# Attention heads scored singly in 32x32 tiles, the last tokens of four heads packed into one tile, values spread through DRAM, softmax sums by half, no instruction padding

## The chip, the cores and the metric

The kernel runs on one core of one Trainium2 chip. The metric is the device time of one execution in microseconds (us). A core has a matrix engine (TensorE, PE in the profile, with its weight loads as PEld), a vector engine (DVE), an activation engine (ACT), GpSimd (POOL), and a queue-only engine (SyncE, SP) that issues most DMAs here. Each engine runs its own instructions in order and waits for the others on semaphores. Matmuls write to PSUM, the accumulation memory, and the other engines read it there; a bank in this text is a stretch of 512 float32 columns, the last dimension of the code's PSUM tiles. Everything else lies in SBUF, 128 partitions wide.

## The reference

Four blocks, each added to its own input: attention A, gMLP B, A, B, all on 2048 tokens of 512 features in bfloat16.

```python
def _A_ref(x, mem0, Wq, Wk, Wv, Wo, seg_len):       # H, Dh = 32, 128;  M, seg = 8, 32
    mask = (idx[:, None] < M) | (idx[:, None] >= idx[None, :])
    mem = mem0
    for s in range(n_seg):                           # 64 segments
        h = jnp.concatenate([mem, x[:, s * seg_len:(s + 1) * seg_len, :]], axis=1)   # 40 rows
        q, k, v = (jnp.einsum('btd,dhe->bhte', h, W) for W in (Wq, Wk, Wv))
        scores = jnp.einsum('bhqe,bhke->bhqk', q, k) * Dh ** (-0.5)
        p = _softmax(jnp.where(mask[None, None], scores, -1000000000.0), axis=-1)
        o = jnp.einsum('bhqk,bhke->bhqe', p, v)
        o = jnp.einsum('bhte,hed->btd', o, Wo)
        mem = o[:, :M, :]                            # the memory of the next segment
        outs.append(o[:, M:, :])
x = x + _A_ref(_layernorm(x), A_mem0, A_Wq, A_Wk, A_Wv, A_Wo, A_seg_len)
x = x + _B_ref(_layernorm(x), B_w_in, B_w_sp, B_b_sp, B_w_out)
x = x + _A_ref(...)
x = x + _B_ref(...)
```

The eight memory rows of a segment's output are the first eight rows of the next segment's input, so the 64 segments of an A block run strictly one after the other. That is 128 segments in all. `_B_ref` (a gelu, a layernorm, a 2048x2048 product over tokens and an output product) is not touched by the change.

## The kernel before

**A segment.** `a_block` runs `segment(s, ...)` 64 times. A segment has 40 rows: 8 of memory, 24 first tokens and 8 last tokens. Only 32 of them pass through the segment's own projections: the memory and the first 24 tokens, transposed in `hA`. The last 8 tokens do not depend on the memory as inputs, so their queries, keys and values are computed ahead for the four segments of a 128-token block at once, 32 rows at a time in `hB`. These are `QTB`, `KTB` and `VB` ("old" or "front" in the profile's names, after the buffers that hold them).

The 32 heads are handled as two halves, r=0 and r=1, of 16 heads. In this order on PE:

- q0 and k0 (`qk`, L690, PSUM tile `psm`): 16 pairs of weight load and matmul each, in tiles of 128x32. ACT casts the result to rows (L867), DVE transposes the rows to `QQ` and `KA` (L871).
- q1 and k1 (`qk_halves`, L880, `psm2`) in two halves of 256 columns each, every half in a PSUM tile of its own; casts L883, transposes L886.
- v0 (`v_mm`, `psV`), cast to `VA` by DVE (L960).
- scores (`scores`, L904), one PSUM tile `psS` for each r. Two heads share a 64-column tile, so each matmul also computes the products of one head's keys with the other's queries, which the mask removes. Per r there are 8 matmuls with `KA` (80 columns) and 8 with `KTB` (32 columns); the 32 rows of `KTB` are the last tokens of all four segments of the block, of which the mask keeps the right ones.
- `exps` (ACT, L911, 448 columns for each r) and `close` (DVE, L914), which multiplies by the 0/1 mask `maskN`.
- v1, cast to `VA` by ACT (L971), and fill units (below).
- The softmax sums: matmuls of `E` with ones. `psM` (L976) has those of the memory rows, `psD` (L985) those of the tokens. Between them stands PV for r=0 (`pv`, L930) into its tile `psO`; PV for r=1 follows in another `psO`.
- Division as Exp(-Ln(sum)) on ACT: `Rm` from psM (L989, L990), `Rt` from psD (Ln L995, 1024 columns; Exp L1003, 512 for each r).
- DVE scales the memory rows of psO by `Rm` into `uT` (L997); the output pass `wo_pass` (L747, 32 heads x 4 tiles = 128 pairs) multiplies `uT` by Wo into `pw`.
- `tok_out` (L944) and `last_out` (L948) scale the token rows by `Rt`. They go to the next segment's `uT` and to a buffer of last tokens, so a segment's tokens pass Wo with the next segment's memory rows.
- `build_hA`: DVE puts the memory rows of `pw` into the next input (copy_predicated, L820) and transposes it to `hA` (L821), which releases the next q0. `store_o` copies `pw` out (L826) and stores it (L827).

**Fill units.** Work that does not depend on the memory stands in the gaps of a segment: `b_units` (the last tokens' projections for the next block) and `y_part` (the last tokens' output product). `fill()` issues the next unit. There are two calls after v1, one before the output pass and one after it.

**Padding.** A page of PE instructions is taken as 256 (`PE_PAGE`). `fills_of` and `pads_of` split matmuls of the projections into two halves of the columns until each segment has 3 x 256 PE instructions, a weight load and a matmul counting as one each.

**Order.** PE, DVE and ACT run in the order in which the code issues the work (`manual_schedule` with `ORDERED`). PSUM tiles come from tagged pools with one buffer each: `accA`, `accB`, `att`, and `attO[0]`, `attO[1]`; a new tile of a tag waits until the one before it has been read.

**SP.** The layernorm rows of a later block go to DRAM and back in other shapes (`rows.apply`: L202 `xn_d`, L205 `preB` x4, L212 `pre` x4), `ln_x` is loaded (L192), `o_sb` is stored (L827), and finished rows are added to x: `y_load` (L220, L222), `y_add` on DVE, `y_norm` with its store (L237).

Of the kernel before, what the change touches and what calls it, by code (L numbers as in the profile page):

```python
# [14 lines left out]
P = 128  # L15
DM = 512
KT = 4
# [11 lines left out]
PE_PAGE = 256  # L29
SEGMENT_PE = 600  # L30
FILL_AHEAD = ((0, 0, 0, 106), (0, 0, 0, 50))
OLD_SIZES = (H * P, 8 * DH, H * 32, H * 32)
ORDERED = {mybir.EngineType.PE, mybir.EngineType.DVE, mybir.EngineType.Activation}

# [21 lines left out]
def _consts(ctx, tc, c, b_sp):  # L56
# [13 lines left out]
    maskf = tmp.tile([P, 4, 112], F32, name="maskf")  # L70
    nc.gpsimd.memset(maskf[:], 0.0)
    for g in range(2):
        for sl in range(2):
            q = 32 * (2 * g + sl)
            nc.gpsimd.memset(maskf[q:q + 32, :, 40 * sl:40 * sl + 40], 1.0)
            nc.gpsimd.memset(maskf[q:q + 32, :, 80 + 16 * sl:96 + 16 * sl], 1.0)

            blk = maskf[q:q + 32, :, 40 * sl + 8:40 * sl + 32]
            nc.gpsimd.affine_select(out=blk, in_=blk, compare_op=ALU.is_ge, fill=0.0, base=8,
                                    pattern=[[0, 4], [1, 24]], channel_multiplier=-1)  # L80

            for lo, step in ((8, 1), (0, 0)):
                blk = maskf[q:q + 32, :, 80 + 16 * sl + lo:88 + 16 * sl + lo]
                nc.gpsimd.affine_select(out=blk, in_=blk, compare_op=ALU.is_ge, fill=0.0, base=0,
                                        pattern=[[-8, 4], [0, 8]], channel_multiplier=1)
                nc.gpsimd.affine_select(out=blk, in_=blk, compare_op=ALU.is_ge, fill=0.0, base=0 if step else 7,
                                        pattern=[[8, 4], [step, 8]], channel_multiplier=-1)
    maskN = cp.tile([P, 4, 112], BF16, name="maskN")
# [5 lines left out]
    for g in range(2):  # L94
        nc.vector.memset(onesG[64 * g:64 * g + 64, g, :], 1.0)
# [378 lines left out]
def kernel(  # L474
# [32 lines left out]
    rows = _Rows(nc, rp, xd, xn_d, xb_d, o_d, x_in)  # L507
    with tc.manual_schedule(engines=ORDERED):
# [89 lines left out]
class _Ahead:  # L598
# [12 lines left out]
    def chunks(self, two):  # L611
# [3 lines left out]
        VB = VB.rearrange("p (r n) -> p r n", r=2)  # L615
        for pair in ((0, 2), (1, 3), (4, 5)):
# [7 lines left out]
            for k, j in enumerate(pair):  # L624
                if j >= 4:
                    nc.scalar.copy(VB[:, j - 4, :], ps[:, k, :])
                    continue
                r = self.rows.pool.tile([P, DM], BF16, name="ln_xn", bufs=2)
                nc.scalar.copy(r[:], ps[:, k, :])
                nc.vector.transpose(out=(QTB, KTB)[k][:, 512 * (j % 2):512 * (j % 2) + 512], in_=r[:])  # L630
# [3 lines left out]
def a_block(tc, c, rows, front, MV_in, RS_in, MV_out, RS_out, ahead, wo, S, first):  # L634
# [6 lines left out]
    with ExitStack() as ctx:  # L641
# [4 lines left out]
        for i in range(2):  # L646
            at, v = 0, list(front.old()) if i == 0 else []
            for n in OLD_SIZES if i == 1 else ():
                v.append(old.tile([P, n], BF16, name=f"old{at}")[:])
                at += n  # L650
            oBr[i] = v[0].rearrange("p (h t) -> p h t", h=H)
            VBr[i] = v[1].rearrange("p (r i e) -> p r i e", r=2, i=4)
# [12 lines left out]
        attO = [_Tagged(ps_pool, f"attO{r}", 1) for r in range(2)]  # L665
# [10 lines left out]
        def mm_chunk(ps, lhs, rhs, kts=range(KT), halved=0):  # L676

            for kt in kts:
                for cg in range(4):
                    k, r = 4 * kt + cg, rhs(kt, cg)  # L680
                    n = halved * (k + 1) // 16 - halved * k // 16
                    o = ps[32 * cg:32 * cg + 32, :]
                    if n and len(r.shape) == 4:
                        parts = [(o.rearrange("p (a b) -> p a b", a=2)[:, a].rearrange("p (i c) -> p i c", i=2), r[:, 2 * a:2 * a + 2]) for a in range(2)]
                    elif n:
                        parts = [(o[:, 256 * a:256 * a + 256], r[:, 256 * a:256 * a + 256]) for a in range(2)]
                    else:
                        parts = [(o, r)]
                    for a, (o, r) in enumerate(parts):
                        nc.tensor.matmul(o, lhsT=lhs(kt, cg), rhs=r, start=(kt == 0 and a == 0), stop=(kt == KT - 1 or halved > 0),  # L690
                                         tile_position=(0, 32 * cg), skip_group_check=halved > 0)
# [4 lines left out]
        QQr = [pers.tile([P, 2, 16, 40], BF16, name=f"QQ{i}") for i in range(NKQ)]  # L696
        uT = [pers.tile([P, H, 32], BF16, name=f"uT{i}") for i in range(2)]
# [5 lines left out]
        def ln_turn(tb):  # L703
            blk_state[tb] = dict(hB=ahead.turn(tb), KTB=KTBr[tb % 2], QTB=QTBr[tb % 2], VB=VBr[tb % 2])


# [8 lines left out]
        def b_units(tb, early=False):  # L715
            bs = blk_state[tb]

            for k, j in enumerate((0, 2, 1, 3, 4, 5)):
# [10 lines left out]
                def out(k=k, j=j, ps=ps):  # L729
                    if j >= 4:  # L730
                        nc.scalar.copy(bs["VB"][:, j - 4].rearrange("p i e -> p (i e)"), ps)
                        return
# [10 lines left out]
        def wo_pass(po, lhs, heads=range(H)):  # L743
            for h in heads:
                n = h // 8 * 8 + 2 * (h % 4) + h // 4 % 2
                for cg in range(4):
                    nc.tensor.matmul(po[32 * cg:32 * cg + 32, 0:128], lhsT=lhs[:, n, :], rhs=wo_rhs(h, cg),  # L747
                                     start=(h == 0), stop=(h == H - 1), tile_position=(0, 32 * cg))
# [6 lines left out]
        def wo_last(parts, pwB):  # L755

            for k, units in enumerate(parts):
                for t, (src, h) in enumerate(units):
                    n = h // 8 * 8 + 2 * (h % 4) + h // 4 % 2
                    nc.tensor.matmul(pwB[32 * t:32 * t + 32, :], lhsT=src[:, n, :], rhs=wo.head(h).rearrange("p (kt g el) -> p g kt el", kt=4, g=4),  # L760
# [49 lines left out]
        def prep_segment(s):  # L810
# [4 lines left out]
            seg_state[s] = dict(QQ=QQ, KTB=bs["KTB"], VB=bs["VB"])  # L815
# [13 lines left out]
        def fills_of(s):  # L829

            if s < 0:
                return FILL_AHEAD[not first]
            if s % 4 == 0:
                return (8, 8, 16, 32) if s // 4 > 3 else (0, 0, 0, 0)
            return (8, 8, 16, 32)

        def pads_of(s):

            n = (3 * PE_PAGE - SEGMENT_PE - fills_of(s - 1)[3] - sum(fills_of(s)[:3]) + 1) // 2
            pads = dict(q0=0, k0=0, q1=16, k1=16, v0=0, v1=0)  # L840
            n -= 32
            for chunk, most in (("k0", 8), ("v0", 8), ("v1", 8), ("v0", 16), ("k0", 16), ("v1", 16), ("q0", 16)):
                k = min(n, most - pads[chunk])
                pads[chunk] += k
                n -= k
            assert n == 0
            return pads

        def segment(s, fill, spare1, spare2, tail):
            tb, j4 = s // 4, s % 4  # L850
            pads = pads_of(s)
            st = seg_state.pop(s)
            QQ, KTB, VB = st["QQ"], st["KTB"], st["VB"]
# [7 lines left out]
            E = segp.tile([P, 2, 4, 112], BF16, name="E")  # L861

            def qk(j):
                ps = (accB if j < 2 else accA).tile([P, 512], F32, name="psm")
                mm_chunk(ps, lambda kt, cg: hA_cur[:, kt, :], lambda kt, cg: qk_rhs(w, j, kt, cg), halved=pads[("q0", "q1", "k0", "k1")[j]])
# [303 lines left out]
```

## Time and profile before

| | |
|---|---|
| median of 3 runs (lowest, highest) | 1766.57 us (1764.97, 1771.19) |
| span of the profiled execution | 1737.3 us |
| PE busy | 1682.0 us, 97% |
| PEld busy | 1271.2 us, 73% |
| DVE busy | 1167.4 us, 67% |
| ACT busy | 1111.3 us, 64% |
| POOL busy | 121.4 us, 7% |
| DMA queue q1: packets, MB, share of 16 engines | 182728, 90.38, 21.2% |

The span is the time from the first to the last instruction of one profiled execution; the medians are of whole executions and include what lies around it. Busy time is the time in which an engine has at least one instruction under way. Matmuls are pipelined, so rows of the timeline overlap, and the start of a row says more than its length. In a row of a timeline stand: start in us, length in us, engine, line, operation, output<-input by the program's names, shapes, and how many instructions are grouped (x); in brackets the idle time before and what released the engine. In the rows of the waits view stand the waiting engine, tile and line, what it waited for, then the sum in us, the number of times and the longest.

### The profile page before, as it was taken

How to read it: one execution, taken by the hardware profiler on the slowest of the kernel's cores; microseconds unless marked ns; L12 is line 12 of the kernel's file. 1: busy time of each engine (PE TensorE's matmuls, PEld its weight loads, DVE VectorE, ACT ScalarE, POOL GpSimd, SP SyncE). 2: the span in 40 equal slices, each digit the busy share in tenths (PEclk: the TensorE clock that was granted, in tenths of full speed). 3: DMA queues.
4: the chain of work that ended last, by engine and by line, in shares of the span. 5: the costliest groups of instructions: out<-in, count | busy, mean ns of one | idle time of the engine just before them, and what ended most of it. 6: DMA issues, size and time to landing. Idle time of an engine off the chain costs nothing.

```text
span 1737.3 us, 109678 instructions
## 1 busy us (share of the span) xinstructions
PE 1682.0 (97%) x51110; PEld 1271.2 (73%) x51110; DVE 1167.4 (67%) x2880; ACT 1111.3 (64%) x2274; POOL 121.4 (7%) x272
## 2 busy tenths in 40 slices
PE   2999999999999999999999999999999999999999
PEld 1677777777777777766667777777777777776565
DVE  2666777777777876784466667667777677667722
ACT  1677777777777777662047777777777777766500
POOL 6000000000000000021100000000000000001100
PEclk9999999999999999999999999999999999999999
DMA  9201000012001201277940000001210022114696
GB/s 352 74 21 21 21 21 21 20 54 63 18 21 50 73 25 38 72 186 154 214 142 23 24 24 24 24 23 30 75 57 24 24 82 64 32 29 145 147 196 161
DMA packets 191793, 124.53 MB, mean 72 GB/s; under 512 B 135872, under 2 KB 167984, under 8 KB 191336
## 3 DMA queue, kind: packets, MB, share of 16 engines
q1 hardware_dynamic: 182728, 90.38, 21.2%
q0 software_dynamic: 8592, 27.12, 4.6%
q8 instruction: 399, 6.54, 1.6%
q14 instruction: 58, 0.48, 0.1%
q10 hardware_dynamic: 16, 0.01, 0.0%
HBM read 57.06 MB, written 33.53 MB: 52 GB/s over the span
## 4 chain that ended last, share of the span: by engine, by line
PE 94%; DMA 2%; DVE 2%; POOL 1%; issue 1%; ACT 0%; SPq 0%; DVEq 0%; POOLq 0%
PE psV L690 13%; PE psm L690 13%; PE pw L747 13%; PE psm L880 13%; PE psb L690 9%; PE pg L384 8%; PE psS L904 5%; PE psO L930 4%; PE pz L283 4%; PE pwB L760 3%; PE py L427 2%; PE psD L985 2%; PE psM L976 2%; DMA Wo_high<-in_A_Wo_dram 1%; DMA Wv_sb<-in_A_Wv_dram 1%
## 5 line engine op out<-in xcount | busy, mean ns | idle before, releaser
L690 PEld LDWEIGHTS <-hA 128*32 128x32 bf16 x10964 | 357.5, 96 | 145.0 <-DVE hA L821 54.2
L690 PE MATMUL psV<-Wv_sb,hA 128*32 128x256 bf16 (+1 forms) x5795 | 280.5, 318 | 0.4 <-issue 0.2
L747 PEld LDWEIGHTS <-uT 128*32 128x32 bf16 x16384 | 231.4, 97 | 46.2 <-DVE uT L997 41.6
L880 PEld LDWEIGHTS <-hA 128*32 128x32 bf16 x8192 | 237.0, 97 | 0.8
L867 ACT CAST rows<-psm 128x512 bf16<-128x512 f32 x256 | 150.1, 586 | 127.2 <-PE psm L690 127.2
L944 DVE TENSOR_TENSOR uT<-psO,Rt 128x384 bf16<-128x384 f32 x256 | 140.7, 550 | 111.8 <-ACT Rt L1003 111.6
L883 ACT CAST rows<-psm 128x256 bf16<-128x256 f32 x512 | 191.2, 374 | 16.8
L911 ACT ACTIVATE E<-psS 128x448 bf16<-128x448 f32 x256 | 125.4, 541 | 116.7 <-PE psS L904 116.7
L997 DVE TENSOR_TENSOR uT<-psO,Rm 128x128 bf16<-128x128 f32 x256 | 62.4, 286 | 161.8 <-PE psO L930 161.8
L1003 ACT ACTIVATE Rt<-Rt 128x512 f32<-128x512 f32 x256 | 157.4, 629 | 4.0
L384 PE MATMUL pg<-z,wspT 128*128 128x344 bf16 x1024 | 154.3, 309 | 0.0
L690 PE MATMUL psm<-Wk_sb,hA 128*32 128x256 bf16 (+1 forms) x3121 | 141.1, 306 | 5.9 <-issue 2.5
L747 PE MATMUL pw<-Wo_high,uT 128*32 128x128 bf16 x8704 | 145.0, 219 | 0.8 <-DMA Wo_high<-in_A_Wo_dram 0.8
L690 PE MATMUL psm<-Wq_sb,hA 128*32 128x512 bf16 x2048 | 134.0, 382 | 8.0 <-DVE hA L821 7.6
L384 PEld LDWEIGHTS <-wspT 128*128 128x128 bf16 x1024 | 100.2, 98 | 53.2
L747 PE MATMUL pw<-Wo,uT 128*32 128x128 bf16 x7680 | 133.6, 219 | 4.3 <-DVE uT L997 3.0
L880 PE MATMUL psm<-Wk_sb,hA 128*32 128x256 bf16 x4096 | 137.0, 273 | 0.0
L880 PE MATMUL psm<-Wq_sb,hA 128*32 128x256 bf16 x4096 | 136.9, 273 | 0.0
L914 DVE TENSOR_TENSOR E<-E,maskN 128x448 bf16<-128x448 bf16 x256 | 104.6, 411 | 36.5 <-ACT E L911 34.4
L995 ACT ACTIVATE Rt<-psD 128x1024 f32<-128x1024 f32 x128 | 128.8, 1007 | 0.0
L690 PEld LDWEIGHTS <-hB 128*32 128x32 bf16 x2976 | 80.5, 97 | 54.3 <-DVE hB L605 26.1
L871 DVE STREAM_TRANSPOSE QQ<-rows 128x512 bf16<-128x512 bf16 x128 | 88.9, 694 | 34.3 <-ACT rows L867 34.3
(173 smaller groups left out, 2756.8 us busy)
## 6 DMA issues: line engine op xcount, KB each, us to landing
o_d<-o_sb SPq DMA_DIRECT2D x126, 64.0 KB
ln_x<-xd SPq DMA_DIRECT2D x26, 256.0 KB
y_o<-o_d SPq DMA_DIRECT2D x22, 256.0 KB
xd<-y_o SPq DMA_DIRECT2D x22, 256.0 KB
y_x<-xd SPq DMA_DIRECT2D x22, 256.0 KB
Wq_sb<-in_A_Wq_dram POOLq DMA_DIRECT2D x8, 512.0 KB, 6.7
Wk_sb<-in_A_Wk_dram POOLq DMA_DIRECT2D x8, 512.0 KB, 10.5
Wv_sb<-in_A_Wv_dram POOLq DMA_DIRECT2D x8, 512.0 KB, 11.5
```

Source lines behind the costliest of these rows:

```text
L384: nc.tensor.matmul(pg[t][:, k, 0:344], lhsT=wsp[t][:, st, :], rhs=z(st, 344 * k, 344 * k + 344), start=(st == 0), stop=(st == NT - 1))
L690: nc.tensor.matmul(o, lhsT=lhs(kt, cg), rhs=r, start=(kt == 0 and a == 0), stop=(kt == KT - 1 or halved > 0), tile_position=(0, 32 * cg), ...
L747: nc.tensor.matmul(po[32 * cg:32 * cg + 32, 0:128], lhsT=lhs[:, n, :], rhs=wo_rhs(h, cg), start=(h == 0), stop=(h == H - 1), tile_position ...
L867: nc.scalar.copy(r[:], ps[:])
L871: nc.vector.transpose(out=QQ[:, j % 2, :, 0:32] if j < 2 else KA[:, j % 2], in_=r[:])
L880: nc.tensor.matmul(ps[32 * cg:32 * cg + 32, 0:256].rearrange("p (i c) -> p i c", i=2), lhsT=hA_cur[:, kt, :], rhs=qk_rhs(w, j, kt, cg)[:, ...
L883: nc.scalar.copy(r[:, 256 * a:256 * a + 256], ps[:, 0:256])
L911: nc.scalar.activation(out=E[:, r], in_=pS, func=ACT.Exp, scale=scale)
L914: nc.vector.tensor_tensor(out=E[:, r], in0=E[:, r], in1=maskN[:, j4, :].unsqueeze(1).to_broadcast([P, 4, 112]), op=ALU.mult)
L944: nc.vector.tensor_tensor(out=hview(uT_nxt[:], r, 8, 32), in0=oview(r, 8, 32), in1=r_view(r)[:, :, :, 0:24], op=ALU.mult)
L995: nc.scalar.activation(out=Rt[:], in_=psD[:], func=ACT.Ln)
L1003: nc.scalar.activation(out=rt, in_=rt, func=ACT.Exp, scale=-1.0)
```

## The change

- **Scores.** Each head has a tile of its own, 32 columns wide (`KA`, 40 query columns): 16 matmuls per r. The last tokens' keys of four heads, 8 each, are packed into one 32-column tile `KX`, multiplied with 64 columns of queries: 4 matmuls per r. `E` has 224 columns per r instead of 448. `KX` is filled by a second copy on POOL in `prep_segment`. Both r share one two-bank tile `psS`, and both halves' scores are issued ahead of the exps.
- **PV.** 32-row tiles: 16 matmuls with `VA` and 4 with `VX` per r. `VX` holds the last tokens' values in the packed order. It is made by `spread_v`: one DMA of `VB` to DRAM and 16 loads back, on SP, once per 128-token block, when the second `VB` chunk has been cast.
- **Sums.** `sums_1` (r=1, `psM`) and `sums_0` (r=0, columns 320 to 480 of `psO`) replace `psM` and `psD`. PV of both r lies in the same four-bank tile `psO`. `Rm` and `Rt` are made for each r: four logarithms and two Exps ahead of the output pass, two Exps behind it.
- **Projections.** q1 is one piece (`psm1`); k1 remains in halves, but both halves and v0 lie in one four-bank tile `psK`, in banks 0, 1 and 2.
- **Order.** The output pass runs the heads of r=1 first (`WO_ORDER`); `_place` gives a head's new place in `uT`. Fill units: one after v1, two before the output pass, one after it. `b_units` begins with the values.
- **Padding.** `PE_PAGE`, `fills_of`, `pads_of` and the `halved` argument are gone.

```diff
-        attO = [_Tagged(ps_pool, f"attO{r}", 1) for r in range(2)]
+        attO = _Tagged(ps_pool, "attO", 1)
...
+        def spread_v(bs):
+            nc.sync.dma_start(rows.vb_d[:], bs["VB"].rearrange("p i r e -> p (i r e)"))
+            for j in range(4):
+                for gs in range(4):
+                    t0 = 32 * gs + 8 * j
+                    nc.sync.dma_start(bs["VX"][32 * gs:32 * gs + 32, j].rearrange("p r e -> p (r e)"),
+                                      rows.vb_d[t0:t0 + 8, :].rearrange("k (i c) -> i k c", i=4))
...
-            for k, j in enumerate((0, 2, 1, 3, 4, 5)):
+            for k, j in enumerate((0, 2, 1, 3, 4, 5) if early else (4, 0, 5, 2, 1, 3)):
...
-                        nc.scalar.copy(bs["VB"][:, j - 4].rearrange("p i e -> p (i e)"), ps)
+                        nc.scalar.copy(bs["VB"][:, :, j - 4, :], ps.rearrange("p (i e) -> p i e", i=4))
+                        if j == 5:
+                            spread_v(bs)
...
+            KX = KXr[s % NKQ]
+            nc.gpsimd.tensor_copy(KX[:].rearrange("p g r (i k) -> p r i g k", i=4).rearrange("p r i g k -> p (r i) g k"),
+                                  bs["KTB"].rearrange("p r (i g) k -> p (r i) g k", i=4)[:, :, :, 8 * j4:8 * j4 + 8])
...
             def scores(r):
+                pS = psS[:, r, :]
+                for i in range(4):
+                    for g in range(4):
+                        n = 4 * i + g
+                        nc.tensor.matmul(pS[32 * g:32 * g + 32, 40 * i:40 * i + 40], lhsT=KA[:, r, n, :], rhs=QQ[:, r, n, :],
+                                         start=(i == 0), stop=True, tile_position=(0, 32 * g), skip_group_check=True)
+                for g in range(4):
+                    q = QQ[:, r].rearrange("p (i g) q -> p i g q", i=4)[:, :, g, :]
+                    nc.tensor.matmul(own(pS[32 * g:32 * g + 32, 160:224]), lhsT=KX[:, g, r, :], rhs=ends(q),
+                                     start=False, stop=True, tile_position=(0, 32 * g), skip_group_check=True)
...
+            def pv(r, ps):
+                for i in range(4):
+                    for g in range(4):
+                        nc.tensor.matmul(ps[:, g, 160 * r + 40 * i:160 * r + 40 * i + 40], lhsT=VA[32 * g:32 * g + 32, r, i, :],
+                                         rhs=E[32 * g:32 * g + 32, r, 40 * i:40 * i + 40], start=False, stop=True,
+                                         tile_position=(32 * g, 0), skip_group_check=True)
+                for g in range(4):
+                    nc.tensor.matmul(ends(heads40(ps[:, g, 160 * r:160 * r + 160])), lhsT=VX[32 * g:32 * g + 32, j4, r, :],
+                                     rhs=own(E[32 * g:32 * g + 32, r, 160:224]), start=False, stop=True,
+                                     tile_position=(32 * g, 0), skip_group_check=True)
...
-            q1, k1 = qk_halves(1), qk_halves(3)
-            for g in (q1, q1, k1, q1, k1, k1):
-                next(g, None)
-            psV = attO[1].tile([P, 512], F32, name="psV")
-            v_mm(0, psV)
+            r1 = qk(1, att.tile([P, 512], F32, name="psm1")[:])
+            psK = attO.tile([P, 4, 512], F32, name="psK")
+            k1 = k_halves(psK)
+            next(k1)
+            qk_T(1, r1)
+            next(k1)
+            next(k1, None)
+            v_mm(0, psK[:, 2, :])
...
-            pS = [scores(r) for r in range(2)]
+            psS = att.tile([P, 2, 512], F32, name="psS")
+            for r in range(2):
+                scores(r)
             for r in range(2):
-                exps(r, pS[r])
+                exps(r)
...
+            psM = att.tile([P, 2, 512], F32, name="psM")
+            sums_1(psM)
+            psO = attO.tile([P, 4, 512], F32, name="psO")
+            sums_0(psO)
+            Rm = segp.tile([P, 2, 128], F32, name="Rm", bufs=1)
+            log_of(Rm, 1, 0, 8)
+            inverse(Rm, 1)
+            for r in range(2):
+                pv(r, psO)
+            log_of(Rm, 0, 0, 8)
+            inverse(Rm, 0)
+            fill(2)
             Rt = segp.tile([P, 2, 512], F32, name="Rt", bufs=1)
+            for r in (1, 0):
+                log_of(Rt, r, 8, 40)
+            for r in (1, 0):
+                scaled(hview(uT_cur[:], r, 0, 8), oview(r, 0, 8), Rm, r, 0, 8)
             pw = accB.tile([P, 512], F32, name="pw")
             wo_pass(pw, uT_cur)
```

Here `log_of` is ACT's Ln of the sums, `inverse` ACT's Exp(-x), and `scaled` DVE's multiplication of a part of psO by a part of Rm or Rt.

## The prediction

> **What bounds the kernel now.** I read the page first: shares, queues, chain.
>
> ```profile
> span 1737.3 us, 109678 instructions
> ...
> q8 instruction: 399, 6.54, 1.6%
> ...
> PE 94%; DMA 2%; DVE 2%; POOL 1%; issue 1%; ACT 0%; SPq 0%; DVEq 0%; POOLq 0%
> ```
>
> TensorE (PE) is the chain for 94% of the span: what leaves it idle is paid in full, and what shortens another engine is worth nothing. The span is 1737.3; the median 1766.57 lies 29.3 outside it, which I add at the end. In the PE's timeline I took every start of `psm<-Wq_sb,hA` as the start of a segment. Of 125 periods (the first segment, 21.0 us of waits for loads, apart) the mean is 11.01 and the shortest common value 10.79. One clean segment, 338.06 to 348.84:
>
> ```profile
> 338.06 1.05 PE L690 MATMUL psm<-Wq_sb,hA 128*32 128x512 bf16 x16
> ...
> 340.67 1.06 PE L880 MATMUL psm<-Wk_sb,hA 128*32 128x256 bf16 x32
> 341.54 1.06 PE L690 MATMUL psV<-Wv_sb,hA 128*32 128x512 bf16 x24
> 342.53 0.23 PE L904 MATMUL psS<-QQ,KA 128*64 128x80 bf16 x2
> ...
> 343.17 1.06 PE L690 MATMUL psV<-Wv_sb,hA 128*32 128x512 bf16 x20
> ...
> 345.70 0.61 PE L690 MATMUL psb<-Wv_sb,hB 128*32 128x512 bf16 x8
> 346.14 1.01 PE L747 MATMUL pw<-Wo,uT 128*32 128x128 bf16 x60
> ```
>
> The second column overlaps from row to row, so starts are what counts: a projection chunk takes .87, v0 to the first score has a gap of .11 where the tile shape changes, the 128 pairs of weight load and matmul of the output pass (L747) take 1.79, that is 14.0 ns a pair. No row here waits: PE streams. The other engines follow behind it:
>
> ```profile
> 340.52 1.63 ACT L883 CAST rows<-psm 128x256 bf16<-128x256 f32 x4
> 343.01 0.98 ACT L911 ACTIVATE E<-psS 128x448 bf16<-128x448 f32 x2 [0.87 <-PE psS L904]
> ...
> 344.92 0.38 ACT L989 ACTIVATE Rm<-psM 128x256 f32<-128x256 f32 x1
> 345.34 0.42 ACT L990 ACTIVATE Rm<-Rm 128x256 f32<-128x256 f32 x1
> 345.66 1.01 ACT L995 ACTIVATE Rt<-psD 128x1024 f32<-128x1024 f32 x1
> ```
>
> ```profile
> 345.79 0.49 DVE L997 TENSOR_TENSOR uT<-psO,Rm 128x128 bf16<-128x128 f32 x2 [1.04 <-PE psO L930]
> ```
>
> Four half casts ride behind four PSUM tiles of their own, and uT starts at 345.79 beside the long logarithm L995 that began at 345.66: the output pass needs only Rm, not Rt.
>
> **The waits of the changed program.** The diff changes which tiles share a name, and a wait is built per tile, not per bank. The waits built into the changed kernel are: (1) the second half of k1 waits for the ACT cast of the first, and v0 for the cast of the second, since all three write one tile psK, though to different banks; (2) the first exp waits for both halves' scores (one psS); (3) the logarithm of Rm for r=0 waits for the last PV matmul, since its sums lie in psO; (4) uT waits for both logarithms of Rt, since ACT reads psO for the r=0 one; before, uT waits only for PV and Rm's Exp. That a read by one engine waits for a read by another is not new; before has it for pw:
>
> ```profile
> ACT o_sb L826 <- DVE pre L820: 30.1, 56, 1.3
> ```
>
> **The sum for one segment**, against 10.79.
>
> *Front.* From a chunk's last issue to its cast's start is .23 (q0 ends .87, L867 starts 1.10), a 256-column cast is .37 (L883), from another engine's end to PE's start .06. Second half of k1: pause .23+.37+.06 = .66, and .04 more since ACT is still at q1's whole cast (.59). v0: .66. Together +1.36. Behind PE's wait stand v0, the scores and all else in order; nothing of a fill is placed there, so nothing hides it. Bounds: the 128-column row .27 (2 x .10 less), the 512-column row .59 (2 x .22 more); I take .37, the same shape.
>
> *Middle.* Scores: 32 pairs in 64-column tiles with a shape gap on either side, .76 from v0's end to v1, become 40 pairs of 32 columns, as wide as the chunks', at 14 ns, .56: -.20. Between v1 and the sums lay 8 fill pairs and a gap, .55; now 4 fill pairs and the masks: two exps of 224 columns (between the .27 and .37 rows, .35 each) and two masks of about .22 end .23 after v1; with the .11 gap .32: -.23. Sums and PV were 44 matmuls in 1.03, now 16+40 at 14 to 16 ns with overheads 1.01: no difference. Total -.43. The KX copy on POOL (7% busy) and the new head order cost nothing while POOL idles; without that cover it is one small copy in front of QQ's, under .5.
>
> *Back.* PV's end to the output pass was .51 (8 fill pairs cover it). Now: PV's end .23 to ACT; Ln Rm0 .27; Exp Rm0 .31 (L990's .42 is 256 columns, this 128); Ln Rt 512 columns .59, then the second, back to back with .10 overlap each, .49 more net of it; two uT of .29, of which the first gates: .03+.29+.06. In order .24+.27+.34-.10+.59+.49+.38 = 2.21. The 12 fill pairs (.73 with gap) hide under it. So +1.70. Bounds: 1024 columns in one row is 1.01 against my 1.08; four-bank strided views have no row, -.1 to +.3.
>
> Sum 1.36-.43+1.70 = 2.63, a period of 13.4; bounds 2.1 and 2.95. The end (output pass, L820, L821, next q0: 2.7) stays.
>
> **Pages.** 6.54 MB in 399 packets is 256 instructions a packet. The padding kept a segment at 768 instructions, three pages; now 736 and drifting. What a page costs PE when late:
>
> ```profile
> 460.30 0.83 PE L690 MATMUL psm<-Wk_sb,hA 128*32 128x512 bf16 x18
> 461.42 0.41 PE L690 MATMUL psm<-Wk_sb,hA 128*32 128x512 bf16 x6 [0.29 <-issue]
> ```
>
> Over all packets: a fetch starts about 1.1 after PE's sequencer enters the page before, lasts 1.08, and the page can be used 1.40 later: 3.58 us for a page. Three make 10.74, just under 10.79, hence such pauses, .09 a segment. At 13.4 a page lasts 4.7, so they nearly vanish. The mean exceeds the clean period by .22: these .09, and .13 of small waits for work that ACT and DVE have only in some segments, which the new pauses mostly take in. I let .07 stand (.03 pages, .04 the rest; 0 to .22), so the mean grows by 2.63-.15 = 2.48. Over 127 segments +315.
>
> The Trainium skill, "Runtime: NRT & Kernel Launch", section Instruction fetch mechanics, says the sequencer fetches the next page while it runs the current one and that the crossing is mostly hidden. The pause above (.58 on the weight loads) shows it is not always; by the page alone there would be no .06 to win back, and the sum would be 8 us more.
> The skill's "TensorEngine Tiling (Array Packing)", section Instruction Overhead, puts some 60 cycles on each matmul and warns against tiling a side that is already small, which speaks against this change: an estimate of 25 ns at the 2.4 GHz that "TensorE: Matmul & The Clock Gate" gives, so 20 more matmuls cost .5 a segment, 64 us in all. The 14.0 ns row decides against it.
>
> **SP.** `spread_v` puts 17 DMAs on SP once per 128 tokens, ahead of o_d, xb_d and a y_o load in four places (two per attention block, j4=2 of tb 7 and 11).
>
> ```profile
> 346.53 2.67 SPq L205 DMA_DIRECT2D preB<-xn_d  x4
> ```
>
> That is .67 an issue for 32 partitions; o_d is .53. 17 issues are 9.0 to 11.4. y_o then lands 25 to 28 after that segment's start; y_add on DVE is due at 13.4+7.4 = 20.8 and can slip 3 (until uT at 23.8) before wo is late: 2 to 5.3 each, +15 in all. While PE pauses that long its clock may halve:
>
> ```profile
> 39.00:42.00 3.00, 0.00 (x0) 0.00 (x0) 0.00 (x0) 0.00 (x0) 2.72 (x4) 0.76 1.05 348
> 42.00:44.00 2.00, 1.86 (x40) 1.31 (x43) 0.50 (x2) 1.02 (x2) 1.01 (x3) 0.50 1.03 339
> ```
>
> (columns: window, length, busy of PE, its loads, DVE, ACT, POOL, then the granted clock). After a 4.57 us pause it was .50 for 5 us; pauses of .83 and less kept 1.00. Four such stalls: +8 (0 to 10). The usual pause here, 1.5, lies between; I count it as 0. At the start the first VX spread stands behind the weight loads: 0 to 12, +6.
>
> Sum: 315+15+8+6 = 344. Span 1737.3+344 = 2081, with the 29.3 outside it 2110. Bounds: 127 x 2.1 = 267 (2033) to 127 x 2.95+43 (2185).
>
> **Rivals.**
> *One of the two groups of waits does not bite* (front or back). For: ACT is 64% busy, so it may reach its work sooner than I stack it; against: in each the wait is on the work just issued. Front alone 1.36-.43+.29 (output pass .80 after PV, from fill length) = 1.22, back alone 1.27: 155 to 161, plus 25: about 1950.
> *Neither bites, PE streams.* 10.79-.43+.29 = 10.65, with .22 of excess and up to .28 of unpadded page loss 10.87 to 11.15 against 11.01: -18 to +18, and SP 30, start 6: about 1803. For: 94% PE chain; against: the built waits.
> *Faster: instruction supply sets the pace.* Three pages of 3.58 are 10.74, and the floor is 10.79; with 2.875 pages a segment falls to 10.3, mean 10.55: 127 x -.46 = -58, SP +24, start +6: 1740. Place: every page crossing; it decides if the period falls under 10.72. For: the pause before 461.42; against: it takes casts that nobody waits for, and the built waits say otherwise.
> *Longer chain*: strided ACT rows dearer than bounds, 2220.
>
> **How the numbers follow.** Forecast .76 (own range 2030 to 2190), one group 1950 .09, streaming 1803 .06, supply 1740 .05, longer .04. 1940 to 2190 holds .76 and half of the second: .8. This kernel's measurement tells about 0.3% (5 us) from no change: faster .05, same .01, slower .94.
>
> **What would show it.** Right: segment periods near 13.4; a pause of .7 before the second half of k1 (`psK`) and again before v0, both released by ACT's cast; wo about 2.2 after PV's end, uT released by ACT's logarithm; PE's share under 82%; fewer "issue" pauses; four stalls of 2 to 5 by y_o. Wrong: k1's halves back to back, uT beside the logarithms, periods under 11.5, or a clock under 1 in the middle of a block (a 1.5 pause then costs more than itself).

## The result, and the profile after

| | before | after |
|---|---|---|
| median (lowest, highest) | 1768.82 us (1764.97, 1771.19) | 2100.23 us (2093.84, 2106.03) |
| ratio, 95% interval | 1 | 1.1877 (1.1839, 1.1916) |
| span of the profiled execution | 1737.3 | 2104.3 |
| clean segment; mean of the ordinary ones | 10.79; 11.01 | 12.98; 13.58 |
| four segments with a late load | none | 21.2 to 21.6 |
| first segment | 21.0 | 33.7 |

The clean segment, called the floor from here on, is what the quickest twentieth of the ordinary segments take. The change makes the kernel 18.8% slower. The page of the changed kernel, span and chain:

```profile
span 2104.3 us, 106502 instructions
...
PE 58%; ACT 22%; DVE 13%; DMA 3%; issue 3%; SPq 0%; POOL 0%; DVEq 0%; POOLq 0%
```

PE had 94% of the chain; now 35 of 100 parts of it are work of ACT and DVE, which before ran behind PE. Where, the timeline of PE in one ordinary segment (681.62 to 694.83) shows:

```profile
684.22 0.61 PE L859 MATMUL psK<-Wk_sb,hA 128*32 128x256 bf16 x16
685.36 0.62 PE L859 MATMUL psK<-Wk_sb,hA 128*32 128x256 bf16 x16 [0.53 <-ACT rows L862]
686.45 1.05 PE L678 MATMUL psK<-Wv_sb,hA 128*32 128x512 bf16 x16 [0.47 <-ACT rows L862]
687.31 0.28 PE L886 MATMUL psS<-QQ,KA 128*32 128x40 bf16 x16
...
687.64 1.06 PE L678 MATMUL psV<-Wv_sb,hA 128*32 128x512 bf16 x16
...
689.69 0.83 PE L678 MATMUL psb<-Wv_sb,hB 128*32 128x512 bf16 x12
691.89 1.08 PE L746 MATMUL pw<-Wo_high,uT 128*32 128x128 bf16 x64 [1.36 <-DVE uT L948]
```

Sixteen pairs of k1 take .44, so the second half could start at 684.66; it starts at 685.36. v0 could start at 685.80 and starts at 686.45. The output pass starts 2.20 after the first of the fill pairs behind PV (689.69). This segment is .23 longer than the floor, at its end, where it waits for the next input. The same places in ACT's and DVE's timeline, and the sums in the waits view (in all, times, longest):

```profile
686.03 0.37 ACT L862 CAST rows<-psK 128x256 bf16<-128x256 f32 x1 [0.72 <-PE psK L859]
...
690.45 0.58 ACT L942 ACTIVATE Rt<-psM 128x512 f32<-128x512 f32 x1
690.92 0.59 ACT L942 ACTIVATE Rt<-psO 128x512 f32<-128x512 f32 x1
```

```profile
691.54 0.49 DVE L948 TENSOR_TENSOR uT<-psO,Rm 128x128 bf16<-128x128 f32 x2 [2.13 <-ACT Rt L942]
```

```profile
DVE uT L948 <- ACT Rt L942: 336.2, 124, 15.6
...
PE psK L859 <- ACT rows L862: 67.3, 128, 0.9
PE psK L678 <- ACT rows L862: 60.2, 128, 0.5
```

uT needs nothing of Rt, and it starts 30 ns after the second logarithm of Rt ends (691.51). uT waits for that logarithm in 124 segments, and the two waits for a cast stand in all 128.

### The profile page after: what moved, and what is told of

Read it like the earlier page. It is cut to its first block, busy times and chain, and to the rows that moved or that the text cites. A ratio compares the mean times of both kernels' runs of the same rounds, so it can differ in the third digit from the quotient of the medians.

```text
span 2104.3 us, 106502 instructions
## 1 busy us (share of the span) xinstructions
PE 1686.2 (80%) x48827; PEld 1041.7 (50%) x48850; DVE 1170.6 (56%) x2754; ACT 1083.8 (52%) x2530; POOL 164.4 (8%) x388
## 4 chain that ended last, share of the span: by engine, by line
PE 58%; ACT 22%; DVE 13%; DMA 3%; issue 3%; SPq 0%; POOL 0%; DVEq 0%; POOLq 0%
PE pw L746 13%; PE psm L678 9%; PE pg L381 7%; PE psK L678 6%; ACT Rt L942 6%; ACT rows L862 5%; DVE KA L850 4%; PE psK L859 4%; PE pz L280 4%; PE psb L678 3%; ACT Rm L945 3%; ACT Rm L942 3%; ACT rows L846 3%; DVE E L897 2%; DVE uT L948 2%
## 5 line engine op out<-in xcount | busy, mean ns | idle before, releaser
L678 PEld LDWEIGHTS <-hA 128*32 128x32 bf16 x10240 | 266.2, 96 | 337.3 <-issue 104.6
L678 PE MATMUL psm<-Wq_sb,hA 128*32 128x512 bf16 x4096 | 277.2, 382 | 12.2 <-DVE hA L822 7.6
L859 PE MATMUL psK<-Wk_sb,hA 128*32 128x256 bf16 x4096 | 161.4, 273 | 67.3 <-ACT rows L862 67.3
L850 DVE STREAM_TRANSPOSE QQ<-rows 128x512 bf16<-128x512 bf16 x256 | 180.8, 706 | 41.6 <-ACT rows L846 35.2
L678 PE MATMUL psK<-Wv_sb,hA 128*32 128x512 bf16 x2048 | 134.0, 380 | 60.2 <-ACT rows L862 60.2
L859 PEld LDWEIGHTS <-hA 128*32 128x32 bf16 x4096 | 112.4, 96 | 119.3 <-issue 93.3
L827 ACT COPY o_sb<-pw 128x128 f32<-128x128 f32 x126 | 33.5, 266 | 225.7 <-DVE pre L821 222.6
L862 ACT CAST rows<-psK 128x256 bf16<-128x256 f32 x256 | 96.0, 375 | 92.3 <-PE psK L859 92.2
L678 PE MATMUL psm<-Wk_sb,hA 128*32 128x512 bf16 x2048 | 137.6, 381 | 2.5 <-DVE yB L775 2.5
L678 PE MATMUL psV<-Wv_sb,hA 128*32 128x512 bf16 x2048 | 136.1, 382 | 0.0
L968 DVE CAST VA<-psK 128x512 bf16<-128x512 f32 x128 | 88.5, 691 | 85.4 <-PE psK L678 85.4
L864 DVE STREAM_TRANSPOSE KA<-rows 128x256 bf16<-128x256 bf16 x256 | 108.5, 424 | 41.5 <-ACT rows L862 41.3
```

The costliest lines, as they stand in the source:

```text
L678: nc.tensor.matmul(ps[32 * cg:32 * cg + 32, :], lhsT=lhs(kt, cg), rhs=rhs(kt, cg), start=(kt == 0), stop=(kt == KT - 1), tile_position=(0, ...
L850: nc.vector.transpose(out=QQ[:, j % 2, :, 0:32] if j < 2 else KA[:, j % 2], in_=r[:])
L859: nc.tensor.matmul(o[32 * cg:32 * cg + 32].rearrange("p (i c) -> p i c", i=2), lhsT=hA_cur[:, kt, :], rhs=qk_rhs(w, 3, kt, cg)[:, 2 * a:2 ...
L862: nc.scalar.copy(r[:, 256 * a:256 * a + 256], o)
L864: nc.vector.transpose(out=KA[:, 1, 8 * a:8 * a + 8], in_=r[:, 256 * a:256 * a + 256])
L968: nc.vector.tensor_copy(VA[:, 0].rearrange("p i e -> p (i e)"), psK[:, 2, :])
```

## The experiments

Each kernel was compared with the kernel before on the same chip; ratios are to that. All but the two marked so start from the changed kernel. The median of the kernel before lay between 1762.75 and 1768.82 us beside them, so a few us between two of these kernels mean nothing.

**The two groups of waits, one at a time and together.** First the front: k1's halves and v0 in three PSUM tiles.

```diff
-            psK = attO.tile([P, 4, 512], F32, name="psK")
-            k1 = k_halves(psK)
+            k1 = k_halves([lambda p=p: p.tile([P, 512], F32, name="psK") for p in (attO, accB)])
...
-            v_mm(0, psK[:, 2, :])
+            psV = accA.tile([P, 512], F32, name="psV")
+            v_mm(0, psV)
```

> The changed kernel with the two halves of k1 and v0 in three PSUM tiles of their own (attO, accB, accA) instead of one; nothing else. Theory (waits per PSUM tile set the pace): the pauses of .67 and .66 us ahead of the second half of k1 and of v0 go, and the scores are next to wait, for DVE's last transpose of the keys, some .4 to .5 later than PE would come; net .8 to 1.3 a segment, 100 to 165 us over 127 segments: 1935 to 2000 us. Rival (the pauses are hidden anyway, the back of the segment decides): no change, 2085 to 2105.

Measured: 1959.51 us, ratio 1.1089 (1.1046, 1.1133). The floor of the period falls from 12.98 to 11.88, the mean from 13.58 to 12.38. PE in a segment of this kernel:

```profile
596.92 1.05 PE L859 MATMUL psK<-Wk_sb,hA 128*32 128x256 bf16 x32
597.79 1.04 PE L678 MATMUL psV<-Wv_sb,hA 128*32 128x512 bf16 x16
598.65 0.27 PE L886 MATMUL psS<-QQ,KA 128*32 128x40 bf16 x16
598.76 0.20 PE L890 MATMUL psS<-QQ,KX 128*32 128x64 bf16 x4
598.86 0.55 PE L886 MATMUL psS<-QQ,KA 128*32 128x40 bf16 x16
```

k1 and v0 run through. Of the two pauses, some .2 comes back: the scores of the second half (598.86) wait for the last transposes of the keys, so their 16 pairs last .55 where those of the first half last .27. That wait is half of what was expected. The theory holds, the rival falls.

The back, one ACT instruction moved:

```diff
-            for r in (1, 0):
-                log_of(Rt, r, 8, 40)
+            log_of(Rt, 1, 8, 40)
             for r in (1, 0):
                 scaled(hview(uT_cur[:], r, 0, 8), oview(r, 0, 8), Rm, r, 0, 8)
+            log_of(Rt, 0, 8, 40)
```

> The changed kernel with one ACT instruction moved: the logarithm of Rt for r=0 is issued after the two multiplications into uT instead of before them. Theory: uT then waits for Rm alone, the output pass starts .4 to .5 us after the last PV and fill work instead of 1.7, 1.1 to 1.3 less a segment, 140 to 165 us, and the halved clock in some segments goes as the pause gets short, 20 to 30 us more: 1900 to 1945. Rival (ACT's work as such is the chain, wherever the logarithm stands): the wait moves to the token outputs and the next segment's start, under 30 us gained, 2070 or more. Both edits together gave 1856: if each alone gains what is said here, the two overlap by what page pauses take back in a shorter segment.

Measured: 1992.79 us, 1.1276 (1.1225, 1.1328): 107 less, under what was expected, and far from the rival. The floor does fall by 1.15, to 11.84. But the mean is .84 above it; in the changed kernel it was .60. DVE and PE of one segment of this kernel show what came in its place:

```profile
646.95 0.63 DVE L948 TENSOR_TENSOR uT<-psO,Rm 128x128 bf16<-128x128 f32 x2 [0.81 <-ACT Rm L942]
```

```profile
647.29 1.08 PE L746 MATMUL pw<-Wo_high,uT 128*32 128x128 bf16 x64
648.20 0.83 PE L746 MATMUL pw<-Wo,uT 128*32 128x128 bf16 x45
649.88 0.40 PE L746 MATMUL pw<-Wo,uT 128*32 128x128 bf16 x15 [0.85 <-issue]
```

uT now starts 30 ns after ACT's logarithm for Rm of r=0 ends (646.92), and the output pass follows at once. That logarithm is again a read of psO: the Rm of r=1, which the first uT uses, had been ready since 646.62. In the middle of the pass PE stops for .85 although its data are there. What it waits for is the next page of instructions: in this trace PE has 90 pauses of over .15 that no engine and no load of data ended, 74.1 us, and 89 of them end 1.15 to 1.65 after a 16 KB packet of instructions has landed (here one landed at 648.64). Of moments picked at random one in ten would. The changed kernel has 21 of these pauses, 14.7 us: while PE waited for ACT, the fetch had time to get ahead.

Both edits:

> Both edits. Theory: the two waits are in series, so the gains add: 1740 to 1830 us; what is left over the kernel before is the start (some 12 us), four stalls by a late load on SP (some 8 us each) and page pauses that come back when the segment gets as short as 10.5 us. Rival (one chain hides behind the other): no better than the better of the two alone, 1900 or more.

Measured: 1856.36 us, 1.0528 (1.0509, 1.0548). Against the changed kernel that is 244 less, and the two alone are 141 and 107: they add, so the waits stand in series. The expected 1740 to 1830 was missed. The floor is 10.75, but the mean 11.55, .80 above it, with four segments of 20.4 to 22.5 still there. PE has 89 pauses of the kind just counted, 67.7 us, where the changed kernel has 14.7. One of them, again in the output pass:

```profile
301.12 0.51 PE L746 MATMUL pw<-Wo,uT 128*32 128x128 bf16 x21 [1.05 <-issue]
```

**The spreading of the values.** First what the four long segments are, in the changed kernel: SP's and DVE's rows in the one from 470.65.

```profile
470.40 10.99 SPq L702 DMA_DIRECT2D VX<-vb_d  x16
...
482.59 0.64 SPq L219 DMA_DIRECT2D y_o<-o_d  x1
```

```profile
485.77 0.69 DVE L223 TENSOR_TENSOR y_o<-y_o,y_x 128x512 f32<-128x512 f32 x1 [7.77 <-DMA y_o<-o_d]
```

Sixteen loads take 10.99 of SP, .69 each. The load of finished rows behind them is issued at 482.59, and DVE stands 7.77 for it, with uT and so the output pass queued behind.

```diff
-            nc.sync.dma_start(rows.vb_d[:], ...)
+            nc.gpsimd.dma_start(rows.vb_d[:], ...)
...
-                    nc.sync.dma_start(bs["VX"]...)
+                    nc.gpsimd.dma_start(bs["VX"]...)
```

> The changed kernel with the 17 DMAs of the values' spreading issued by POOL instead of SP. Theory: the load of finished rows is no longer queued behind them, so the four segments of 21.5 us fall to 13 to 15, 25 to 33 us less, and the first segment loses part of its 12 us: 2055 to 2075. Rival (the late load is late by DMA traffic or by its own place on SP): the four long segments stay and the time is within 10 us of the changed kernel's. A third way: POOL's copies of QQ and KX for the next segment now queue behind the spreading and PE waits for them at the scores: slower, 2110 or more.

Measured: 2048.20 us, 1.1620 (1.1603, 1.1638), 52 less than the changed kernel, somewhat more than expected. After the first, no segment is over 16.1; the mean of the ordinary ones is 13.37, some of it by fewer halved clocks (8 segments, where the changed kernel has 17). The first segment stays at 32.6, so the 12 us that it has gained are not SP's queue. PE there, in the changed kernel:

```profile
56.00 0.23 PE L926 MATMUL psO<-E,VX 32*128 32x64 bf16 x1 [6.46 <-DMA VX<-vb_d]
```

The write of the first values to DRAM is issued at 48.83 and the first load back at 53.71, while the last weight loads still fill the DMA engines; PV waits for them, on either queue. That the weight loads are what makes the way through DRAM so long was not tested.

**The clock.** Apart from the waits, 17 ordinary segments were 1.8 longer than the floor. In the windows view (length, busy of PE, its loads, DVE, ACT and POOL, the clock, the busy share of DMA, GB/s) three stretches around one of them:

```profile
112.65:116.06 3.41, 1.28 (x105) 1.18 (x105) 1.05 (x3) 3.19 (x8) 0.00 (x0) 1.00 0.01 3
116.06:119.48 3.42, 2.69 (x94) 2.15 (x84) 1.20 (x5) 0.27 (x1) 0.00 (x0) 0.50 0.02 5
119.48:122.90 3.42, 3.42 (x40) 1.28 (x36) 1.17 (x4) 0.90 (x2) 0.00 (x0) 0.50 0.09 24
```

The records change the clock in steps of 3.41 us. In the first window PE was busy for 1.28 of 3.41, and the next two ran at half. Counted over the windows from 40 us on that ran at the full clock themselves: after one busy for under half the next was halved in 11 of 11 cases, between .5 and .6 in 9 of 40, above that in none of 521. A window that is halved already can be followed by another at a higher share, as the second row shows (2.69 of 3.42 busy). The pause behind the first row is this one; the second is the usual one, ahead of another halved window:

```profile
115.27 1.23 PE L746 MATMUL pw<-Wo_high,uT 128*32 128x128 bf16 x64 [2.12 <-DVE uT L948]
```

```profile
1320.75 1.75 PE L746 MATMUL pw<-Wo_high,uT 128*32 128x128 bf16 x64 [1.37 <-DVE uT L948]
```

The clock fell 15 times in ordinary segments: 5 times behind a pause of 2.1 to 2.3, in segments without fill work, and 10 times behind a pause of 1.4 to 1.6, as nearly every segment has, where it lay with nearly its whole length in one window. Two experiments give PE needless work in the pause ahead of the output pass. The first has 24 small pairs:

```diff
+            warm = accB.tile([P, 512], F32, name="warm")
+            for kts in (range(KT), (0, 3)):
+                mm_chunk(warm[:], lambda kt, cg: hA_cur[:, kt, :], lambda kt, cg: v_rhs(w, 1, kt, cg), kts)
             pw = accB.tile([P, 512], F32, name="pw")
```

> The changed kernel with 24 pairs of needless matmuls (a projection nobody reads) in the pause ahead of the output pass; all of the computation is kept. Reading of the trace: in windows of 3.41 us in which PE was busy for under half the clock was halved in the next one, in windows over .6 never; 17 of the ordinary segments lose 1.8 us each by it. If that is the cause, more work in the pause makes the kernel faster: no halved clock outside the start and the four stalls, 2060 to 2080 us. Rival (the pause and the clock are both set by something else, or the added work only takes instruction supply): the same or slower, 2095 to 2140.

Measured: 2105.92 us, 1.1943 (1.1923, 1.1964): no gain, a miss, and inside the rival's range. Two ordinary segments touch a halved clock and lose .8 us in all, where the 17 lost 31; but the others' excess rises from .40 to .61, 25 us, and PE's pauses for a page grow from 14.7 to 32.8 us, about half of them in the output pass. That left open whether the halved clock had cost anything. The second experiment brings the busy time with 10 instructions in place of 48:

```diff
+            for k in range(5):
+                nc.tensor.matmul(warm[:], lhsT=ones[:], rhs=wo.head(0), start=(k == 0), stop=(k == 4))
```

> The changed kernel with 5 needless full-width matmuls of 512 columns (10 instructions, some 1.1 us of PE) in the pause ahead of the output pass; all of the computation is kept. With 24 small pairs in that place the halved clock went from the ordinary segments, but 48 more instructions a segment brought page pauses that took the gain back. If that reading is right, the same busy time with 10 instructions keeps the gain: no halved clock in ordinary segments, their other excess over the floor near the changed kernel's .40, 2060 to 2080 us. Rival (the halved clock costs nothing, since those segments are long for another reason): 2095 to 2110.

Measured: 2079.16 us, 1.1764 (1.1736, 1.1792), in the expected range, with an interval wholly under the changed kernel's. No ordinary segment has a halved clock, and the mean excess is .37. PE of this kernel, needless work and output pass:

```profile
112.49 1.25 PE L1001 MATMUL warm<-Wo,ones 128*128 128x512 bf16 x5
114.68 1.08 PE L746 MATMUL pw<-Wo_high,uT 128*32 128x128 bf16 x64 [0.94 <-DVE uT L948]
```

The pass still waits for uT, as it must, but then runs at the full clock: work that nobody reads makes the kernel 1% faster.

**Pages.** Two kernels start from the kernel before. The first is that kernel unchanged:

> The kernel before, unchanged, to see how its span stands to its time. If some 29 us lie outside the span in every execution, span and time differ by 29 here too. If instead its executions differ among themselves, the span lies some 2 us under the time of its own execution.

Measured: ratio 1.000 (.9989, 1.0011), times from 1759.79 to 1766.38, and a span of 1758.7. So nothing like 29 us lies outside a span; the profiled execution of before was itself a quick one. Its mean period is 11.01, here 11.17, and one row of the waits view carries a good part of it. Before, then the same program again:

```profile
PEld L690 <- issue: 25.9, 91, 1.1
```

```profile
PEld L690 <- issue: 40.0, 125, 1.1
```

The weight loads of one and the same program have 91 pauses put down to nothing in one execution and 125 in the other. Not all are for pages: 48 and 74 of them, 16.6 and 28.0 us, end 1.15 to 1.65 after a packet of instructions has landed. The second takes the padding away:

```diff
-            n = (3 * PE_PAGE - SEGMENT_PE - fills_of(s - 1)[3] - sum(fills_of(s)[:3]) + 1) // 2
-            pads = dict(q0=0, k0=0, q1=16, k1=16, v0=0, v1=0)
...
+            pads = dict(q0=0, k0=0, q1=0, k1=0, v0=0, v1=0)
```

> The kernel before without its padding: all chunks in 16 pairs but q1 and k1 in halves as they are, so that a segment has some 40 instructions less than three pages and the page boundary drifts through it; all of the computation is kept. Theory (pages cost only where a boundary meets a short stretch): PE's pauses put down to nothing grow from .09 a segment to at most .28, with the mean period between 10.95 and 11.2: 1760 to 1790 us. Rival (instruction supply sets the pace): a segment falls to 2.84 pages of 3.58, 10.2 to 10.5 us: 1690 to 1720.

Measured: 1789.51 us, 1.0151 (1.0136, 1.0166), slower by 27 us although it has 5,567 instructions less. The mean goes to 11.38, and pauses put to nothing now stand in the output pass (33.5 us there for PE). So fewer pages alone do not make it faster; the two kernels with padding below show what decides.

Next, the two edits and POOL together:

> Both edits to the waits, and the spreading on POOL. Theory: what is left of the change is its packed scores and PV: a floor near 10.4 to 10.8 us a segment with page pauses: 1710 to 1790 us, so it may beat the kernel before. Rival: page pauses and the waits for POOL's copies take the gain back, 1800 or more.

Measured: 1819.59 us, 1.0330 (1.0310, 1.0350). That misses the expected range and lies in the rival's; of the rival's two causes it is the pages: PE has 97 pauses for them, 83.5 us, and waits for POOL's copies in the first segment alone. The floor is 10.63, below the 10.79 of the kernel before and the 10.76 that it has without padding, so the packed scores and PV save about a tenth in a clean segment. The mean is 11.52. To see whether pages are the rest, padding was put back, as a table of split pairs for each segment that holds it at 768 instructions within one:

```diff
+        def pads_of(s):
+            n = PADS[0 if first else 1][s]
...
+                        nc.tensor.matmul(o, lhsT=lhs(kt, cg), rhs=r, start=(kt == 0 and a == 0), stop=(kt == KT - 1 or halved > 0),
+                                         tile_position=(0, 32 * cg), skip_group_check=halved > 0)
```

> Both edits, the spreading on POOL, and padding as in the kernel before: matmuls of the projections split in two until each segment has 768 PE instructions within one, with the page boundary at the same three places of the segment as in the kernel before. Theory (page pauses, .75 to .9 a segment, are what is left): the mean falls from 11.5 to 11.0-11.2 although some 16 more pairs run in each segment, 1755 to 1785 us, and three pages of 3.58 keep it from getting under 10.74. Rival (the left over pauses have to do with the waits for ACT and DVE, not with pages): more instructions make it no faster, 1815 or more.

Measured: 1790.59 us, 1.0132 (1.0090, 1.0173), 29 less with some 16 more pairs a segment. It lies 6 us above the expected range; the mean is 11.30, and PE's pauses for pages have fallen from 83.5 to 33.6 us. The same with the boundary half a page later:

> The same with the page boundary moved by 128 instructions, so that one stands shortly after the output pass begins and the next at the segment's end. Theory (a page must last 3.6 us or PE waits for the next): that page holds the output pass and a fill unit, some 2.7 us, so that PE waits .7 to 1.0 for the next in each segment: 1850 to 1900 us. Rival (only the number of pages counts): as with the boundary of the kernel before, within 10 us.

Measured: 1869.47 us, 1.0585 (1.0544, 1.0627), inside the range. Nearly every output pass now stops at the same place:

```profile
404.36 0.90 PE L758 MATMUL pw<-Wo,uT 128*32 128x128 bf16 x51
406.53 0.34 PE L758 MATMUL pw<-Wo,uT 128*32 128x128 bf16 x9 [1.27 <-issue]
...
416.41 0.89 PE L758 MATMUL pw<-Wo,uT 128*32 128x128 bf16 x50
418.63 0.34 PE L758 MATMUL pw<-Wo,uT 128*32 128x128 bf16 x10 [1.33 <-issue]
```

```profile
PE pw L758 <- issue: 131.8, 125, 2.4
```

All 125 end 1.15 to 1.65 after a packet of instructions has landed. Two kernels with the same work, and but for 64 more split pairs in the first segment the same instructions, differ by 79 us. A last, small shift was to win a tenth a segment:

> The padded best version with the page boundary 8 pairs earlier in the segment. From the starts of its clean segments the three pages last 3.97, 3.24 and 3.49 us now, which is .42 short of 3.58 each, and 3.87, 3.56 and 3.28 with the shift, .32 short (the kernel before: 3.69, 3.64, 3.45, .13 short). Theory: .1 a segment less, 13 us: 1772 to 1783. Rival (differences of a tenth are lost in other pauses): 1786 to 1795. On neither does it beat the kernel before.

Measured: 1793.71 us, 1.0150 (1.0121, 1.0178). No gain; the mean is 11.35. The arithmetic with 3.58 a page came near the wait above (.7 to 1.0 expected, 1.05 measured), but a difference of .1 it could not tell. None of these kernels beats the kernel before.

## Why the prediction was right, and where it was not

**The mechanism.** Of the four built waits that the prediction lists, (1) and (4) stand where it put them, in all 128 and in 124 segments. (2), the first exp behind both halves' scores, is there in all 128 without cost to PE. (3), the logarithm of Rm for r=0 behind PV, shows as a wait in only 21; in the segment above ACT comes to it from the Exp before it without a pause. The front edit, the back edit and both together show that these groups are most of the slowdown (244 of 331 us). The spreading accounts for some 50.

**Front**, +1.36: .70 and .65 in the segment above. Right.

**Back**, +1.70: PV's end (.07 ahead of 689.69) to the output pass is 2.27 here where .51 was before, +1.76. Right.

**Middle**, -.43: from v0's start to the first fill pair after PV it was 341.54 to 345.70, 4.16; now 686.45 to 689.69, 3.24, so -.92. The mis-sized term is the price of a small pair, 14 ns from the output pass. 16 score pairs start within 687.31 to 687.41, 6.4 ns each, and all 40 take .33 instead of .56; sums and PV take some .75 instead of 1.01. In tiles of this width a pair takes 54 ns with 512 columns in the moving operand (16 in .87), 14.0 with 128 and 6.4 with 40; the sum took the 14.0 for all. So the floor is 12.98 (10.79+1.35-.92+1.76), not 13.4. The stated bounds of the sum, 2.1 to 2.95, hold the 2.19 that it measured, but they do not follow from the bounds of its terms, which give 2.33 to 3.37: the middle had none. The overhead that "TensorEngine Tiling (Array Packing)" in the Trainium skill, section Instruction Overhead, gives, at the estimate of 25 ns a matmul that the prediction drew from it, would make the scores alone 1.0 if the matmuls came one after another. Shared among four tiles of 32 columns, the same 25 ns are an estimate of 6 ns a pair, close to the 6.4 measured (16 in .10). The trace has them start in fours, one four every 25 to 28 ns (687.311, 687.339, 687.364, 687.389). So it was the use of the figure that failed, and not the figure.

**Excess over the floor**: .07 was let stand, .60 was measured. Of its 72 us over 121 ordinary segments, 31 lie in 17 segments with a halved clock. The prediction counted the usual pause of 1.5 as 0 and named a lower clock within a block as what would make it wrong; the clock did fall there, 10 times behind such a pause and 5 times behind one of over 2. In the other segments the excess is .40 on average: page pauses, some .12, and the small waits of single segments, which the new pauses did not take in. The page pauses did not nearly vanish, as the prediction has it, nor are they less than in its profile: 14.7 us in 21 pauses, against 3.9 in 13 in the first profile of the kernel before and 9.7 in 32 in the second.

These two errors nearly cancel: the mean grows by 2.57, forecast 2.48. That the sum of ordinary segments came out is partly luck.

**SP**, +15 and +8 for the clock: four segments at 21.46 on average, 7.9 over the mean, 32 in all. Place and price of an issue were right (.69 against .67). In the segment shown the rows arrive 28.3 after the start of the segment before it (457.4), at the upper end of 25 to 28; uT comes 6 later than it would have, and the output pass behind so long a pause runs at half the clock and takes 3.4 instead of 1.8.

**Start**, +6 with bounds 0 to 12: +12.7, above the bound. PV's waits for `VX` are 7.6 of it; the rest is the waits that every segment has now and a longer stretch at half the clock, not taken apart. The second profile of the kernel before has 23.7 in place of 21.0.

**What lies outside the span**, 29.3: wrong. It was the difference between one quick execution and the others; the changed kernel's times lie under 2 us over its spans. From that execution's own span the growth is 367 and the sum was 344; from the second profile of the kernel before (1758.7) it is 346. The forecast of 2110 met 2100 since a sum from a quick execution and an offset that does not exist went together.

**Rivals.** That one group of waits does not bite, or that neither does, is refuted by the two edits. That instruction supply sets a segment's pace, so that fewer instructions make it faster, is refuted by the kernel before without padding, which the rival would have made faster. What was true in it came out when the waits were gone: page pauses hold what both edits could have brought.

## What to carry to other kernels

Before merging accumulators into one PSUM tile, list what the tile's readers then wait for: the wait is built for the tile, so the cast of one bank holds up the matmuls into the next, and a read by ACT that nobody needs yet holds up a read by DVE that everybody waits for. (The front edit shows the first: the halves of k1 lie in different banks. In psO both reads lie in the same four banks, so the back edit does not tell a wait for the tile from one for the bank.) Moving one ACT instruction behind DVE's was worth 107 us. When a wait is taken away, ask what had used it as cover: here the fetch of instructions, so that some .4 of the 2.2 us a segment that both edits freed came back as pauses for pages. And take the span of a kernel's profile twice before counting anything as lying outside it.

## What the runs showed of the hardware

- In a 3.41 us window in which PE is busy for less than about half, the clock of the next window is halved (11 of 11 windows at the full clock in the changed kernel; 9 of 40 between .5 and .6; none of 521 above). It is not exact: in the kernel with the spreading on POOL, 5 of 7 windows under half were followed by a halved one, and one of 221 between .6 and .8. No pause needs to last 3.41 us: one of 2.1 was enough, and 10 times one of 1.4 to 1.6, which most often left the clock alone. Ten needless instructions a segment prevented it.
- "TensorE: Matmul & The Clock Gate" in the Trainium skill, section The HAM clock gate, has the throttled state follow an idle window of about 3.4 us; the trace agrees with the window's length, but the window at 112.65 was 38% busy and still led to a halved clock.
- Whether PE waits for an instruction page depends on which 256 instructions share it: the padded kernel took 1790.59 us with the boundary in one place and 1869.47 half a page later, with 33.6 and 135.7 us of PE's pauses put down to nothing. Over the 14 traces 833 of 846 such pauses of over .15 end 1.15 to 1.65 after a 16 KB packet of instructions has landed.
